# A convolution branch beside a gated MLP, forward and backward: loads and first products reordered, and the tap gradient's halo made by a shift product on TensorE

## Chip, cores and metric

One core of a Trainium2 chip. The metric is the device time of one execution in microseconds (us), lower is better. Time before: 2040.27 us (median of 3 runs, 2038.81 to 2040.48). A *ratio* is the recorded one of two kernels' runs in the same rounds on the same chip, so it is not quite the ratio of the medians that stand beside it, and can differ from that of the plain means in the fourth digit. Medians of different chips differ by some 4 us for the same kernel; the ratios do not carry that.

## The reference, cut

```python
def _A_ref(q, k, v, shift_k, ssm_k, ssm_D):            # "branch A"
    k_pad = jnp.pad(k, ((0, 0), (ks - 1, 0), (0, 0)))
    k_shift = sum over t of k_pad[:, t:t + S, :] * shift_k[:, ks - 1 - t]   # 4 taps
    kv = k_shift * v
    y = irfft(rfft(kv padded to 2S) * rfft(ssm_k padded to 2S))[:S]         # per channel
    y = y + kv * ssm_D
    return q * y

def _B_ref(x, W_gate, W_up, W_down):                   # "branch B", the MLP
    h = relu(x @ W_gate) * (x @ W_up)
    return h @ W_down

xn = _layernorm(x)                                     # over the last axis
out = x + _A_ref(xn, k, v, ...) + _B_ref(xn, ...)
# outputs: out, and the gradients of x, k, v, shift_k, ssm_k, ssm_D, W_gate, W_up, W_down
```

x, k, v are 2048 x 1024, the weights 1024 x 3584, all bf16. Of the gradients one matters here: that of `shift_k` needs, for each of the 4 taps, products of the gradient of `k_shift` with k moved by 0 to 3 positions, and the gradient of k needs the gradient of `k_shift` moved by 0 to 3 positions. A tile holds 16 positions per partition and three more, the **halo**, which belong to the next partition.

## The kernel before: the parts that matter

The MLP is a generator of TensorE work (in `hidden` each block of 512 columns is 24 products of 8 matmuls for half of the rows). Branch A is a second generator, in 8 groups of 128 channels; each `yield ns` says how much MLP work should pass before its next step. A scheduler then orders every engine's instructions by priority (`pri.now()` ahead of `pri.late()`); each engine executes its own list in that order.

```python
    def open(self):                                   # branch A's buffers
        self.ts = self.pool("a_ts", 3, side=R)        # three rotating work buffers: ttile()
        self.ps = self.pool("a_ps", 2, space=PSUM)    # two PSUM buffers for all of branch A
        ...
    def flip(self, src):                              # transposing copy: two halves on VectorE
        for c0 in range(0, 64, 32):
            self.pri.late()
            self.nc.vector.transpose(out=df[:, c0:c0 + 32, :], in_=sf[:, c0:c0 + 32, :])
        return dst
    ...
    def steps(self):
            ...
            yield from self.inv_b(Cg, gkv, 2000)      # gradient of kv
            gks = self.gradients(st, gkv, ksh)
            yield 6000
            yt = self.ttile("yt")
            yield from self.inv_b(Cy, yt, 2000)
            self.store_time(self.y_d, cg, yt)
            yield from self.inv_a(GH, 1800)           # last inverse step (GH,IA), ends in the flip
            Ch = self.flipped
            yield from self.grad_taps(gi, gks, kp, 1800)
            if nx is not None:
                self.loads_2(nx)
            yield 1500
            ghn = self.ttile("ghn")
            yield from self.inv_b_chan(Ch, ghn, 2000) # the flipped product (RB,flp)
    ...
    def gradients(self, st, gkv, ksh):
        gv = self.ttile("gv")
        self.tt(gv[:, 0:16, :], gkv[:, 0:16, :], ksh[:], ALU.mult)
        self.store_time(self.out_gv, cg, gv)
        gks = self.ttile("gks")
        self.tt(gks[:, 0:16, :], gkv[:, 0:16, :], vt[:], ALU.mult)
        pri.late()
        nc.gpsimd.memset(gks[:, 16:19, :], 0.0)                     # the halo:
        self.store(gks[0:64, 16:19, :], gks[64:P, 0:3, :])          # two SBUF-to-SBUF DMAs
        self.store(gks[64:P - 1, 16:19, :], gks[1:64, 0:3, :])
        gk = self.ttile("gk")
        self.taps(st, gk, gks, [(0, 0), (1, 1), (2, 2), (3, 3)])    # 7 passes of VectorE
        self.store_time(self.out_gk, cg, gk)
        return gks
    ...
    # the start
    b.ln_load(x, a.frm, "frm", 0)                     # first tile of x
    first = b.weights(B_W_gate, B_W_up, B_W_down, 0)  # 12 weight loads
    b.layer_norm(x, xn_d, a.frm, "frm", a.tmp, "tmp", a.sm)   # loads the rest of x, pieces of 3, 4, 4, 4
    with tc.issue_after(b.ln_act.ins), tc.issue_after(b.ln_dve.ins):
        a.tables()                                    # Fourier tables, at pri.now()
    ...
    a_steps, left = a.steps(), A_START                # cut: the loop that mixes both generators
```

## Time and profile before

| | before |
|---|---|
| time, median | 2040.27 us |
| span of the profiled execution | 2037.0 us |
| TensorE busy | 1930.9 us (95%) |
| next busiest engine, VectorE | 995.2 us (49%) |
| TensorE waits of the first 80 us: taps table, layer norm, VectorE's tables | 16.1 + 12.2 + 11.4 us |
| TensorE waits for the flip | 17.1 us |

The prediction below shows most of the lines. Two more, from the groups of instructions by shape (line, engine, operation, out<-in, shapes, count, then busy us and mean ns, then idle us of that engine just before them and what ended most of it):

```profile
L65 PE MATMUL ps<-RB,flp 128*128 128x64 bf16 x256 | 10.6, 203 | 16.9 <-DVE flp L281 16.6 <-DVE dg L73 0.2
L69 ACT CAST yt<-ps 128x1024 bf16<-128x1024 f32 x16 | 15.5, 1021 | 3.1 <-DMA out_dram<-gv 2.9
```

The first is the product that waits for the flip. The second is an eviction on ScalarE that waits for a store of `gv`. And the end of the MLP's first block, from TensorE's timeline (start us, length us, what):

```profile
91.38 3.62 PE L576 MATMUL ps_h<-wdT,goT 128*128 128x512 bf16 x15
94.83 3.62 PE L576 MATMUL ps_g<-wg,xnT 128*128 128x512 bf16 x16
```

`ps_g` at 94.83 is the second block's first product. "Block 0 ends at" always means this instant.

### The profile page before, as it was taken

The numbers are of one execution on the slowest core, as the hardware profiler recorded it, in microseconds if no ns is written. First come the engines' busy times: TensorE is split into PE (matmuls) and PEld (weight loads), VectorE is DVE, ScalarE is ACT, GpSimd is POOL, SyncE is SP. The second block draws the span as 40 slices with busy tenths as digits, with TensorE's granted clock in tenths as the row PEclk, the third lists the DMA queues.
The fourth block names the chain that finished last, engine by engine and source line by source line (L and its number), as shares of the span: only waits on it lengthen the run. The fifth ranks groups of instructions, "written<-read, shape, count | busy, mean of one in ns | idle before, by whom it ended". The sixth has DMA issues, their size and how long they took to land. (4 is left out here: it accounts for less than half of the span.)

```text
span 2037.0 us, 27072 instructions
## 1 busy us (share of the span) xinstructions
PE 1930.9 (95%) x10806; PEld 914.7 (45%) x11014; DVE 995.2 (49%) x1444; ACT 690.4 (34%) x902; POOL 20.1 (1%) x46
## 2 busy tenths in 40 slices
PE   4799999999999989999899999999989999999998
PEld 2345445444444445444444544444434444444443
DVE  4848578677687677565575740000112222223332
ACT  6456366356356347474655731111000000000000
POOL 1000000000000000000000000000000000000000
PEclk9899999999999999999999999999999999999999
DMA  9764666865565674545535269332899554454551
GB/s 266 203 160 125 160 159 172 196 174 169 156 167 161 167 192 135 152 131 153 179 119 162 73 169 334 106 119 83 182 257 233 150 134 114 114 126 119 122 128 45
DMA packets 616095, 319.10 MB, mean 157 GB/s; under 512 B 450080, under 2 KB 585248, under 8 KB 615968
## 3 DMA queue, kind: packets, MB, share of 16 engines
q1 hardware_dynamic: 614688, 313.16, 58.5%
q0 software_dynamic: 1280, 4.20, 0.6%
q8 instruction: 86, 1.41, 0.3%
q14 instruction: 41, 0.34, 0.1%
HBM read 141.36 MB, written 95.44 MB: 116 GB/s over the span
## 5 line engine op out<-in xcount | busy, mean ns | idle before, releaser
L673 PE MATMUL ps_w<-ugs,xn_nat 128*128 128x512 bf16 x1746 | 395.3, 380 | 2.7 <-issue 0.5
L673 PEld LDWEIGHTS <-xn_nat 128*128 128x128 bf16 x1792 | 171.5, 98 | 202.9 <-issue 7.1
L576 PEld LDWEIGHTS <-xnT 128*128 128x128 bf16 x1792 | 169.3, 98 | 201.2 <-issue 18.7
L576 PE MATMUL ps_h<-wdT,goT 128*128 128x512 bf16 x865 | 205.7, 382 | 13.4 <-DVE ru L634 11.4
L576 PE MATMUL ps_g<-wg,xnT 128*128 128x512 bf16 x875 | 207.8, 383 | 4.2 <-DVE ru L634 2.6
L576 PE MATMUL ps_u<-wu,xnT 128*128 128x512 bf16 x870 | 205.6, 380 | 1.7 <-issue 0.5
L673 PE MATMUL ps_d<-g_nat,hs 128*128 128x512 bf16 x866 | 203.1, 380 | 4.1 <-DMA ug_d<-ru 1.4
L757 PE MATMUL ps_o<-wd,hT 128*128 128x512 bf16 x878 | 195.0, 382 | 9.8 <-DMA hT<-h_d 8.9
L790 PE MATMUL ps_x<-wgT,ggT 128*128 128x512 bf16 x878 | 197.5, 379 | 1.0
L790 PE MATMUL ps_x<-wuT,guT 128*128 128x512 bf16 x878 | 197.3, 379 | 0.9
L759 DVE TENSOR_TENSOR o<-ps_o,ya 128x512 bf16<-128x512 f32 x32 | 21.5, 687 | 270.4 <-PE ps_o L757 269.8
L711 ACT CAST wi<-ps_w 128x512 bf16<-128x512 f32 x112 | 65.4, 585 | 255.8 <-PE ps_w L673 245.0
L757 PEld LDWEIGHTS <-hT 128*128 128x128 bf16 x896 | 87.7, 98 | 116.9 <-DMA hT<-h_d 10.8
L790 PEld LDWEIGHTS <-ggT 128*128 128x128 bf16 x896 | 87.6, 98 | 105.7
L790 PEld LDWEIGHTS <-guT 128*128 128x128 bf16 x896 | 87.6, 98 | 105.7
L576 PEld LDWEIGHTS <-goT 128*128 128x128 bf16 x896 | 84.9, 98 | 111.7 <-issue 20.2
L646 ACT CAST gh<-ps_h 128x512 bf16<-128x512 f32 x112 | 65.5, 586 | 202.5 <-PE ps_h L576 120.4
L792 DVE CUSTOM_DVE_ANT_0 gx<-ps_x,gy 128x512 f32<-128x512 f32 x32 | 22.1, 691 | 226.6 <-PE ps_x L790 212.5
L673 PEld LDWEIGHTS <-hs 128*128 128x128 bf16 x896 | 82.6, 98 | 98.7 <-issue 9.1
L281 DVE STREAM_TRANSPOSE flp<-B 128x1024 f32<-128x1024 f32 x48 | 90.1, 1934 | 47.8 <-ACT B L69 47.8
L634 DVE SCALAR_TENSOR_TENSOR ru<-ru,ps_u 128x512 bf16<-128x512 bf16 x112 | 76.0, 680 | 73.8 <-PE ps_u L576 47.9
L69 ACT CAST B<-ps 128x1024 bf16<-128x1024 f32 x96 | 95.6, 1020 | 36.0 <-PE ps L65 35.8
(152 smaller groups left out, 1707.9 us busy)
## 6 DMA issues: line engine op xcount, KB each, us to landing
ug_d<-ru SPq DMA_DIRECT2D x112, 256.0 KB, 3.4
ugs<-ug_d SPq DMA_DIRECT2D x112, 256.0 KB, 4.7
wg<-in_B_W_gate_dram SPq DMA_DIRECT2D x56, 256.0 KB, 3.4
wu<-in_B_W_up_dram SPq DMA_DIRECT2D x56, 256.0 KB, 4.6
h_d<-ht SPq DMA_DIRECT2D x112, 128.0 KB, 1.7
hs<-h_d SPq DMA_DIRECT2D x56, 256.0 KB, 4.4
out_dram<-wi SPq DMA_DIRECT2D x56, 256.0 KB, 2.1
gt<-in_grad_out_dram SPq DMA_DIRECT2D x32, 256.0 KB, 3.8
```

The source lines that it names most:

```text
L69: self.nc.scalar.copy(out=out, in_=in_)
L281: self.nc.vector.transpose(out=df[:, c0:c0 + 32, :], in_=sf[:, c0:c0 + 32, :])
L576: self.nc.tensor.matmul(ps[:], lhsT=xT[:, kt * P:(kt + 1) * P], rhs=w(kt), start=(kt == 0), stop=(kt == self.DT - 1))
L634: nc.vector.scalar_tensor_tensor(out=ru[s][:, 1, :], in0=ru[s][:, 0, :], scalar=0.0, in1=ps[:], op0=ALU.is_gt, op1=ALU.mult)
L646: nc.scalar.copy(out=gh[:], in_=ps[:])
L673: self.nc.tensor.matmul(ps[:], lhsT=lhsT(st), rhs=rhs(st), start=(st == 0), stop=(st == self.ST - 1))
L711: nc.scalar.copy(out=wo[:, d, :], in_=ps[:])
L757: nc.tensor.matmul(ps[:], lhsT=hT[:, kt, :], rhs=self.wd[:, kt, oc], start=(kt == 0), stop=(kt == self.FT - 1))
L759: nc.vector.tensor_tensor(out=o0[:, oc], in0=ps[:], in1=ya[:, oc], op=ALU.add)
L790: nc.tensor.matmul(ps[:], lhsT=T[:, kt, :], rhs=W[:, kt, oc], start=(i == 0), stop=(i == n - 1))
L792: V.tensor_tensor_reduce(out=gx[:, oc], in0=ps[:], in1=gy[:, oc], scale=1.0, scalar=0.0, op0=ALU.add, op1=ALU.add, accum_out=m[:, ob:ob + 1])
```

## The change

Intent: (1) at the start, issue loads and first products in the order in which they are needed, and give the table building low priority; (2) get the halo of the gradient of `k_shift` by a product with a shifted identity, instead of two DMAs, so that VectorE does not wait for them. Cut to its core:

```diff
     def tables(self):
-        pri.now()
+        pri.late()
 ...
+        self.NX = con.tile([P, P], BF16, name="NX")          # out[m] = in[m+64], from 64 on in[m-63]: the next 16 positions
+        V.tensor_copy(out=self.NX[:, 0:64], in_=self.identA[:, 64:P])
+        V.tensor_copy(out=self.NX[:, 64:P - 1], in_=self.identA[:, 1:64])
 ...
     def grad_taps(self, gi, gks, kp, ns):
-        ps = self.ps.tile([P, 4, 32], F32, name="ps6", tag="aps")
+        ps = self.ps.tile([P, 2, 512], F32, name="ps6", tag="aps")
+        self.mm(ps[:, 1, 0:3 * P], self.NX[:], gks[:, 0:3, :].rearrange("p r c -> p (r c)"))
+        self.act(gks[:, 16:19, :].rearrange("p r c -> p (r c)"), ps[:, 1, 0:3 * P])
 ...
     def steps(self):
             self.store_time(self.y_d, cg, yt)
+            yield from self.grad_taps(gi, gks, kp, 1800)
+            self.grad_k(st, gks)                 # the gk part of gradients(), now after yt
+            if nx is not None:
+                self.loads_2(nx)
             yield from self.inv_a(GH, 1800)
             Ch = self.flipped
-            yield from self.grad_taps(gi, gks, kp, 1800)
-            if nx is not None:
-                self.loads_2(nx)
-            yield 1500
+            yield 5000
             ghn = self.ttile("ghn")
 ...
     def gradients(self, st, gkv, ksh):
         self.tt(gks[:, 0:16, :], gkv[:, 0:16, :], vt[:], ALU.mult)
-        nc.gpsimd.memset(gks[:, 16:19, :], 0.0)
-        self.store(gks[0:64, 16:19, :], gks[64:P, 0:3, :])
-        self.store(gks[64:P - 1, 16:19, :], gks[1:64, 0:3, :])
-        gk = self.ttile("gk")
-        self.taps(...)
 ...
-    LN_CHUNKS = (1, 3, 4, 4, 4)
+    LN_CHUNKS = (1, 1, 2, 4, 4, 4)
 ...                                              # block 0: gate and up products of the first two
+                ahead = fb + half == 0           # tiles come ahead of the first down product
 ...
-    b.ln_load(x, a.frm, "frm", 0)
-    first = b.weights(B_W_gate, B_W_up, B_W_down, 0)
+    load(0)
+    first = [b.col_block(B_W_gate, 0, "wg")]
+    load(1)
+    first.append(b.col_block(B_W_up, 0, "wu"))
+    load(2)
+    load(3)
+    first.append(b.row_block_T(B_W_down, 0, "wdT"))
+    goT = [b.load_T(g, i, "goT") for i in range(4)]
+    load(4)
+    a.load_shift()
+    load(5)
```

Also in it, cut here: the table of square roots is loaded by an activation at the very start, the transpose of the filter taps moves to the start of branch A, and one product of branch A (`gt * xt`) is made later.

## The prediction

> **What bounds the kernel now.** I read the page's table of engines first, then the slices, the waits of TensorE, and the timeline of the stretches where TensorE is idle.
>
> ```profile
> PE 1930.9 (95%) x10806; PEld 914.7 (45%) x11014; DVE 995.2 (49%) x1444; ACT 690.4 (34%) x902; POOL 20.1 (1%) x46
> ...
> PE   4799999999999989999899999999989999999998
> ```
>
> TensorE is busy for 95% of 2037 us; no other engine passes half. Only what shortens TensorE's idle time can pay, and that is 2037.0 - 1930.9 = 106 us at most. About 200 of the 11014 matmuls have no record (10806 against 11014 weight loads; at 0.216 us each, 8 in 1.73 us in the chain, up to 45 us), so the true idle time is nearer 65 to 90 us. The waits and the timeline say where:
>
> ```profile
> PE ps L65 <- DVE flp L281: 17.1, 9, 2.9
> PE ps_sk L205 <- DMA sk_b<-in_A_shift_k_dram: 16.1, 1, 16.1
> PE pst_x L600 <- DVE ln_x L558: 12.2, 2, 10.3
> PE ps_h L576 <- DVE ru L634: 11.4, 2, 10.5
> PE ps_o L757 <- DMA hT<-h_d: 8.9, 4, 3.1
> PE ps L65 <- ACT H L69: 6.0, 7, 2.0
> ...
> 10.35 1.03 PE L600 MATMUL pst_x<-ident,ln_x 128*128 128x128 bf16 x8 [10.35 <-DVE ln_x L558]
> 27.47 0.29 PE L205 MATMUL ps_sk<-identA,sk_b 128*32 128x128 bf16 x1 [16.09 <-DMA sk_b<-in_A_shift_k_dram]
> ...
> 30.41 5.95 PE L576 MATMUL ps_g<-wg,xnT 128*128 128x512 bf16 x16
> ...
> 79.21 0.59 PE L576 MATMUL ps_h<-wdT,goT 128*128 128x512 bf16 x1 [10.51 <-DVE ru L634]
> ```
>
> (columns of a wait: total us, times, longest; of the timeline: start, length, what, the wait before it). Three places concern the change. **The start**: the first real product begins at 30.4 us; before it there are only transposes. The wait charged to the taps table (16.1 us) is not the cause alone: the second piece of x is issued at 12.65 us, behind twelve weight loads, lands at 18.8, and its layer norm ends at 30.3. **At 69 to 79 us** VectorE makes tables for 10 us without a break while two finished products wait for it. **From 200 to 1207 us**, where the convolution branch runs beside the MLP, 28 us of waits remain, 17.1 of them for the flip. The tail (last product at 2028.5) and the 8.9 us for hT are not touched by the change.
>
> **What the Trainium skill says.** "Perfetto Trace Analysis", Identifying the Most-Contended Engine and Optimization Strategy: TensorE's busy share is a poor measure because matmuls are pipelined; look for gaps on the contended engine and for what releases them. The trace agrees: records last 380 ns but come every 216. "ScalarE: Activation LUTs", What ACT_TABLE_LOAD costs: about 1283 ns a load. The trace has 1.28 us three times. "TensorE: Matmul & The Clock Gate", Part 1: after some microseconds of idle the array restarts at half clock. The trace agrees: the first 16 gate matmuls took 5.95 us, later 16 take 3.62, and the stretch 70:80 was granted 0.63. "DMA: Bandwidth & Descriptors", Latency and other measured facts: a DMA has about 2 us of fixed cost. The halo copy in the chain took 2.19 us, but its wait is longer, below.
>
> **Part 1, loads and first products in order of need.** x comes in pieces of 1, 1, 2, 4, 4, 4 tiles; the new issue order is x0, gate, x1, up, x2, x3, down, four goT, x4, x5. The square-root table is loaded while x0 is in flight: its 1.28 us started at 6.72 us in the chain of the first tile, of which about 0.8 is saved. What the diff hides is in the built order of each engine. VectorE copies the first two transposed tiles only after the layer norm of x0, x1 and x2; and ScalarE's first relu comes after all 16 reductions of x0 to x3 and four of x4. So I follow these two queues with durations of the trace (ScalarE 1.04 us a pass over a tile; VectorE 0.43 per tile and subtraction or scaling, about 0.2 per small operation, eight of them after the root).
>
> - x0 lands at 3.48 as before and is normalised at about 9.5; x1 passes through both queues behind it, until 14.7.
> - x2: 3 MB lie ahead of its end. At 250 GB/s (the first two slices have 266 and 203, the first 10 us 253) that is 12 us plus 2 of latency: 14. Two passes on ScalarE to 16.2, subtract, two passes to 19.5, one pass over x3 put between, root at 20.7, eight small operations to 22.3, scaling to 23.2, first copy at 23.9. **The first gate product starts at about 24 us**, not 11 as the new order of loads suggests, against 30.4.
> - Four products of eight matmuls, the first ones cold: to 33.4. The next transposes need a bank that only the relu frees, at 34 to 35. Their copies stand behind the subtraction of x4 and the evictions of the up products: 39.1. So a second gap of about 5 us.
> - From 39 us the block has 20 products of 1.73 us left, 34.6 us, plus some 6 us for two more pairs of transposes behind layer-norm work. The tables are now cut up: MLP operations stand between pieces of at most 1.34 us (2.3 for one), so the 10.5 us gap goes. **Block 0 ends at about 80 us.**
>
> Before, its last products ran from 91.38 to 94.8, and that included 2.0 us of filter transposes now done later. Gain: 94.8 - 2.0 - 80 = **12.8 us**, all on the path, as TensorE is the bound from there on.
>
> **Part 2, the halo.** Removed, eight times: a memset on GpSimd, two SBUF-to-SBUF copies, and VectorE's wait for them:
>
> ```profile
> DVE tap L73 <- DMA gks<-gks: 51.9, 7, 20.7
> ...
> 249.79 0.85 SPq L85 DMA_DIRECT2D gks<-gks  x1
> ...
> 253.24 0.88 SPq L85 DMA_DIRECT2D gks<-gks  x1
> ...
> 255.60 1.23 DVE L73 TENSOR_TENSOR tap<-gks,skb 128x2048 bf16<-128x2048 bf16 x1 [1.06 <-DMA gks<-gks]
> ...
> 265.40 1.88 DVE L281 STREAM_TRANSPOSE flp<-C 128x1024 f32<-128x1024 f32 x1
> ...
> 267.33 1.89 PE L65 MATMUL ps<-RB,flp 128*128 128x64 bf16 x32 [2.65 <-DVE flp L281]
> ```
>
> VectorE's 51.9 us of waiting are not on the path as such: it is 49% busy. The path is their consequence. gks is ready at 226, but the copies are issued only at 249.8 and 253.2, in a queue shared with other traffic; the tap sums then crowd in front of the two flips, and TensorE waits for the second flip. By shapes, 16.6 of the 17.1 us are before this one product (7 or so groups, some 2.3 us each). In the new order the two flips stand ahead of most tap sums, and 24 to 40 MLP matmuls (5 to 9 us) lie between the last inverse step and the flipped product, where 5 to 39 lay before, mostly about 18. I take 14 of the 16.6 as gained. The crowding of convolution steps with 0 to 3 matmuls between them, which gives the ScalarE waits (H 6.0, others near 5), moves to other groups and is a little less: 2 us gained.
>
> Added: eight matmuls of 128x384, 0.216 x 384/512 = 0.16 us and a weight load of 0.10: 2 us at most, 1.5 as they overlap. Their evictions on ScalarE (about 0.5 us each, from 0.6 at 512 columns) lie beside other work on an engine that is 34% busy. The new product waits for gks, with about 60 matmuls (13 us) between its cause and it: no stall. **Sum of part 2: -14 - 2 + 1.5 = -14.5 us.**
>
> Total: 2040.3 - 12.8 - 14.5 = **2013 us**.
>
> **Rivals.** (a) The early start is worth far more: products begin at 11 or 12 us, as x0, x1 and the gate weights are there by 8. For it: the intent, and the flips stand first on TensorE. Against: the built VectorE order. It would gain 10 to 13 us more: about 2001. (b) The start gains nothing, because layer norm on ScalarE (32 passes of 1.04, 33 us, plus relus) or the load of x4 behind eight transposing DMAs bounds both kernels, and waiting moves from before 30 us to 33 to 56. The queues above leave only a few us of slack; then the start gives 3 to 5 us: about 2022. (c) The flip waits are not due to the halo but to the crowding of the scheduler's order; then another wait (ghn's eviction waiting for the last tap sum, or the shift product's bank, shared with the tap product in two buffers, held until ScalarE and VectorE have both read it) takes their place: part 2 gives 3 us, the time is about 2024. (d) Later transfers hide the gain: A finishes earlier or later, but it had 230 us to spare before the weight gradients end at 1437, so this costs nothing.
>
> **Range and chances.** The start is uncertain by some 6 us either way, part 2 by 6 and rearrangement elsewhere by 5: together 10, so 80% lie within about 12 to 13: **2001 to 2027 us**. Faster by over 2% means under 1999.5, 41 us, nearly all the idle time touched here (30 + 12 + 28, less a start that cannot be below 11): chance 0.09. Slower by 2% would take a new stall in every group: 0.01. Within 2%: 0.90.
>
> **What would show it.** Right, if: the first gate product stands at 22 to 26 us with an idle gap of 4 to 8 us near 34 to 39; block 0 of the MLP ends at 76 to 84; no 10 us wait of ps_h on VectorE; the wait of the flipped product is under 4 us in total; no DMA wait before the taps; eight NX products of about 0.2 us without a wait. Wrong, if the gate starts near 12 (then a), or if ScalarE or x4's DMA holds TensorE for over 10 us between 30 and 60 (b), or if waits of the convolution products from 200 to 1200 us still sum to over 20 us (c).

## The result, and the profile after

The changed kernel took **2011.27 us** (median of 4 runs, 2010.59 to 2014.13) beside 2040.38 for the kernel before on the same chip: ratio 0.9861, 95% interval 0.9844 to 0.9879. That is "within 2%", and the predicted 2013.0 is 1.7 us from it. Run again later on another chip (below) the ratio was 0.9848 (0.9832 to 0.9865).

The page after: engines, and TensorE's busy share by fortieth of the span.

```profile
PE 1944.6 (97%) x11022; PEld 916.2 (46%) x11022; DVE 996.6 (50%) x1460; ACT 694.6 (35%) x912; POOL 16.3 (1%) x36
...
PE   3999999999999999999999999999999999999998
```

The slice of 7 tenths and three of 8 have become 9. Busy time *rose* by 13.7 us mainly because this trace has a record of all 11022 matmuls: a later trace of the same kernel (e14 below), with 10817 records, is busy for 1927.8 us. What TensorE waited for:

```profile
PE ps_g L595 <- DVE xnT L621: 11.4, 4, 6.8
...
PE pst_x L619 <- ACT ru L645: 6.1, 1, 6.1
PE ps_o L789 <- DMA hT<-h_d: 5.9, 3, 2.6
...
PE ps L65 <- DVE flp L291: 2.5, 3, 1.3
```

The flip's 17.1 us became 2.5, and the 11.4 us of `ps_h` on VectorE do not occur. The start, from the timeline of both engines concerned:

```profile
24.10 5.67 PE L595 MATMUL ps_g<-wg,xnT 128*128 128x512 bf16 x16 [6.84 <-DVE xnT L621]
...
34.40 1.06 ACT L554 ACTIVATE ln_j<-ln_x 128x1024 bf16<-128x1024 bf16 x1 [4.58 <-DMA ln_x<-in_A_q_dram]
...
38.66 1.05 ACT L645 ACTIVATE ru<-ps_g 128x512 bf16<-128x512 f32 x2
...
39.29 1.86 PE L619 MATMUL pst_x<-ident,ln_x 128*128 128x128 bf16 x16 [6.06 <-ACT ru L645]
...
43.48 6.21 PE L595 MATMUL ps_g<-wg,xnT 128*128 128x512 bf16 x16 [2.33 <-DVE xnT L621]
...
84.93 3.62 PE L595 MATMUL ps_g<-wg,xnT 128*128 128x512 bf16 x16
```

The first gate product stands at 24.10 us (before: 30.41). Then a second gap: ScalarE waits 4.58 us for the fifth piece of x, the relus stand behind its four passes, and only the relus free the PSUM banks for the next transposes. Block 0 ends at 84.93. The product after the flip, and the eight new shift products:

```profile
L65 PE MATMUL ps<-RB,flp 128*128 128x64 bf16 x256 | 10.1, 193 | 1.6 <-DVE flp L291 1.5
...
L65 PE MATMUL ps<-gks,NX 128*128 128x384 bf16 x8 | 2.6, 326 | 0.0
```

From three instants of both timelines the span's 27.6 us (2037.0 to 2009.4) divide as follows. Before, block 0 also held 2.0 us of filter transposes, which the change moves past it; they are taken out of the first row and put into the second.

| stretch | before | after | gain | predicted |
|---|---|---|---|---|
| start to end of block 0 | 94.83 - 2.0 | 84.93 | 7.9 | 12.8 |
| to the end of the weight gradients | to 1437.05 | to 1412.66 | 16.5 | 14.5 |
| output phase to the end | 600.0 | 596.7 | 3.2 | 0 |

The total is right to 2 us partly because misses have opposite signs (-4.9, +2.0, +3.2), which is luck. The first row is also a late case: in six other traces of the same start (e1, e3, e12, e4, e14, e17) block 0 ends at 81.6 to 82.9, a gain of 10.0 to 11.3. And 16.5 in the second row says *where*, not *why*.

### The profile page after: what moved, and what is told of

It reads as the page before. It is cut to its first block, busy times and chain, and to the rows that moved or that the text cites. A ratio compares the mean times of both kernels' runs of the same rounds, so it can differ in the third digit from the quotient of the medians. Undisturbed runs are those within 1.5% of the kernel's fastest.

```text
span 2009.4 us, 27247 instructions
## 1 busy us (share of the span) xinstructions
PE 1944.6 (97%) x11022; PEld 916.2 (46%) x11022; DVE 996.6 (50%) x1460; ACT 694.6 (35%) x912; POOL 16.3 (1%) x36
## 4 chain that ended last, share of the span: by engine, by line
PE 47%; ACT 2%; DMA 1%; SPq 1%; issue 0%; DVE 0%; DVEq 0%
PE ps_x L822 19%; PE ps_w L705 17%; PE ps_o L789 8%; PE ps L65 1%; DMA hT<-h_d 1%; ACT G L69 1%; SPq L781 0%; ACT H L69 0%; ACT K L69 0%; ACT wi L743 0%; ACT B L69 0%; SPq L758 0%; PE pst L280 0%; DVE gx L837 0%; DVE gm L834 0%
## 5 line engine op out<-in xcount | busy, mean ns | idle before, releaser
L705 PE MATMUL ps_w<-ugs,xn_nat 128*128 128x512 bf16 x1792 | 400.2, 379 | 1.1 <-DMA xn_nat<-xn_d 1.0
L595 PE MATMUL ps_g<-wg,xnT 128*128 128x512 bf16 x896 | 213.6, 387 | 15.4 <-DVE xnT L621 11.4
L705 PE MATMUL ps_d<-g_nat,hs 128*128 128x512 bf16 x896 | 208.6, 381 | 3.6 <-DMA hs<-h_d 3.6
L69 ACT CAST C<-ps 128x1024 bf16<-128x1024 f32 x96 | 96.7, 1016 | 48.4 <-PE ps L65 48.4
```

Of the source, the lines that this page charges most:

```text
L69: self.nc.scalar.copy(out=out, in_=in_)
L595: self.nc.tensor.matmul(ps[:], lhsT=xT[:, kt * P:(kt + 1) * P], rhs=w(kt), start=(kt == 0), stop=(kt == self.DT - 1))
L705: self.nc.tensor.matmul(ps[:], lhsT=lhsT(st), rhs=rhs(st), start=(st == 0), stop=(st == self.ST - 1))
```

## The experiments

**Theory** (the prediction's): VectorE's wait for the halo copies pushes the tap sums in front of the flips; the shift product removes it. **Rivals:** the flip waits come from the scheduler's order and the buffers' rotation, so it is the reordering that pays and the shift product is beside the point; and, for the start, that x's later pieces and layer norm bound it. Twelve runs; the ratio is always to the kernel before in the same rounds. All outputs are right.

| run | what it is | median us (lowest to highest) | ratio [95%] | flip wait us | block 0 ends |
|---|---|---|---|---|---|
| e1_start_only | part 1 alone | 2032.69 (2026.70-2034.56) | 0.9947 [0.9934, 0.9960] | 17.5 | 82.5 |
| e2_halo_only | part 2 alone | 2020.54 (2018.93-2023.82) | 0.9894 [0.9881, 0.9907] | 1.1 | 98.4 |
| e3_order_dma_halo | all but the shift product | 2013.71 (2012.01-2016.44) | 0.9860 [0.9847, 0.9872] | 3.1 | 82.9 |
| e12_gk_after_yt | e1 + gk after yt | 2024.35 (2023.59-2025.34) | 0.9911 [0.9896, 0.9925] | 14.0 | 82.5 |
| e4_shift_old_order | e1 + shift product, old order | 2024.53 (2019.19-2028.85) | 0.9934 [0.9920, 0.9949] | 18.6 | 81.6 |
| e6_tables_now | change, tables at high priority | 2018.27 (2017.27-2019.40) | 0.9903 [0.9891, 0.9916] | 2.4 | 90.9 |
| e5_x4_early | change, fifth piece of x earlier | 2007.34 (2006.97-2010.19) | 0.9853 [0.9840, 0.9865] | 2.9 | 80.1 |
| e10_products_first | change, layer norm staged behind products | 2007.50 (2003.74-2011.02) | 0.9850 [0.9837, 0.9864] | 2.5 | 84.5 |
| e14_after_again | the change, unaltered | 2008.31 (2005.22-2009.22) | 0.9848 [0.9832, 0.9865] | 1.4 | 82.2 |
| e17_room_before_flip | e12 + one number | 2007.53 (2007.00-2009.52) | 0.9845 [0.9830, 0.9859] | 2.4 | 81.6 |
| e13_products_first_gp_store | e10 + early stores issued by GpSimd | 1997.47 (1995.14-1997.78) | 0.9791 [0.9776, 0.9806] | 1.1 | 71.4 |
| e15_products_first_gp_store_x4 | e13 + e5 | 1997.17 (1995.45-1998.17) | 0.9791 [0.9777, 0.9806] | 2.4 | 72.2 |

The first four shared one chip (before there: 2042.25), the next four a second (2038.13), the last four a third (2041.08).

### The two halves

`e1_start_only`: the change with the whole halo part (grad_taps, gradients, the order of the steps) as before.

> Part 1 alone: the changed start, with the halo by two copies and the old order of the group's tail. In the trace of the changed kernel block 0 of the MLP ends at 84.9 us against 92.8 before (94.8 less 2.0 of filter transposes moved to later), so the start is worth 7.9 us. Theory (the two parts are independent): 2040.4 - 7.9, a time of 2030 to 2034 us, block 0 ending at 84 to 86, and waits of TensorE for the flip between 200 and 1210 us of 12 to 20 us as before. Rival (the start shifts the branch against the MLP, and that is what thinned the later waits): under 2027 us, flip waits under 8 us.

`e2_halo_only`: the kernel before with the halo part alone.

> Part 2 alone: the old start (with the identity matrix shared, which frees the memory needed), the shift product and the new order of the tail. From the two traces the stretch from the end of block 0 to the end of the weight gradients is 14.5 us shorter although 2.0 us of transposes moved into it, so part 2 should be worth 16.5 us, and 3.1 us came in the output phase, which neither part touches. Theory (independent parts): 2040.4 - 16.5 = 2024, less up to 3 if the output phase's gain belongs to part 2: 2020 to 2025 us, the gap near 70 to 79 us still there. Rival (part 2 gains only with the new start): over 2030 us.

Measured: the start alone gives 0.53%, part 2 alone 1.06%, together 1.59%; the whole change 1.39% and, on another chip, 1.52%. So the parts add, near enough. The 12.0 us of `ps_h` on VectorE stay in e2 and go in e1; the flip's waits stay in e1 (17.5) and go in e2. Each wait belongs to the half it was assigned to. (Block 0 of e1 ended at 82.5, earlier than the expected 84 to 86, which came from the late trace.)

### Is it the shift product?

`e3_order_dma_halo`: the changed kernel, but the halo made by DMA as before.

```diff
-        self.mm(ps[:, 1, 0:3 * P], self.NX[:], gks[:, 0:3, :]...)
-        self.act(gks[:, 16:19, :]..., ps[:, 1, 0:3 * P])
+        self.nc.gpsimd.memset(gks[:, 16:19, :], 0.0)             # in gradients(), as before
+        self.store(gks[0:64, 16:19, :], gks[64:P, 0:3, :])
+        self.store(gks[64:P - 1, 16:19, :], gks[1:64, 0:3, :])
```

> The changed kernel with the shift product taken out again: halo by memset and two copies as before, everything else (order of the tail, yt before gk, wider gap before the last product) as changed. Theory O (the order and the rotation of the three work buffers made the gain, since yt took the buffer of gv and its eviction waited for the late store of gv): within 3 us of the changed kernel, 2008 to 2014 us, waits for the flip under 5 us, although VectorE waits for the halo copies 30 us or more. Rival D (the prediction's: VectorE's wait for the halo copies is what pushed the flips): 2020 to 2026 us with flip waits of 10 us or more.

`e4_shift_old_order`: the reverse. The shift product is there, but `gk` before `yt`, the taps after the inverse step and the 1500 are as before.

```diff
             gks = self.gradients(st, gkv, ksh)
-            yield 6000
+            yield 3000
+            self.shift_halo(gks)          # NX product and its eviction alone
+            self.grad_k(st, gks)
+            yield 3000
```

> Part 1 plus the shift product alone: the halo comes from TensorE right after gks, gk is summed at once as before (so gk is allotted before yt, and yt takes the buffer of gv), tap product after the inverse step, short gap. Theory O (rotation of the buffers): yt's eviction still waits for the late store of gv, the inverse steps and the last product stay bunched (1 to 4 and 5 to 8 matmuls between them in the built order), so the time is that of part 1 alone within 4 us, 2029 to 2036 us, with flip waits over 10 us. Rival D (halo copies were the cause): 2013 to 2020 us, flip waits under 5 us.

Waits of e3, then of e4:

```profile
DVE gk L73 <- DMA out_dram<-gv: 24.6, 5, 11.7
...
PE ps L65 <- DVE flp L287: 3.1, 3, 2.7
...
DVE tap L73 <- DMA gks<-gks: 0.3, 1, 0.3
...
PE ps L65 <- DVE flp L291: 18.6, 9, 2.4
```

Measured: e3 has the ratio of the change itself (0.9860 beside 0.9861 and 0.9848), flip waits of 3.1 us, and VectorE waits for its halo copies 0.3 us in all, where it waited 51.9. (Its tap sums now wait 24.6 us at their start for the store of `gv`, and the copies land meanwhile; the flips do not suffer from that either.) e4 removes the wait for the copies from VectorE just as well (4.1 us for ScalarE's eviction of the halo instead) and still has 18.6 us of flip waits; `yt`'s eviction waits 9.3 us for the store of `gv`, as expected of it. Its time fell between the two expectations; its ratio differs from that of e1, on another chip, by 0.0013, within the intervals. **Taking the halo copies away is neither enough for the gain (e4) nor needed for it (e3), and the shift product is worth nothing that these runs can show.** This refutes the theory.

### Then what in the reordering?

`e12_gk_after_yt`: part 1, halo by DMA, and of part 2 only that `gk` is made after `yt`.

```diff
+            self.grad_k(st, gks)          # was inside gradients(), before yt
             yield from self.inv_a(GH, 1800)
```

> Part 1 alone plus one move: the sum gk is made after yt has been evicted, so that yt takes the buffer of gkv (free after gks) and not that of gv (free only after its store). Halo by copies, tap product after the inverse step and the short gap as before. Theory O: the inverse steps are spread again (8 matmuls between them in the built order, where 1 to 4 stood), yt's eviction shows no wait for the store of gv, flip waits fall below 8 us, time 2013 to 2022 us. Rival D (halo copies): as part 1 alone within 3 us, about 2032 us.

Why that could matter, in the trace of the kernel before (first group; SPq is a DMA issue in SyncE's queue):

```profile
224.85 0.64 SPq L85 DMA_DIRECT2D out_dram<-gv  x1
...
249.06 0.64 SPq L85 DMA_DIRECT2D out_dram<-gv  x1
...
253.40 1.93 ACT L69 CAST yt<-ps 128x1024 bf16<-128x1024 f32 x2 [2.93 <-DMA out_dram<-gv]
```

Three work buffers rotate. With the order gkv, gv, gks, gk, yt, the fourth and fifth take the buffers of gkv and gv, so `yt` waits until gv has been stored; and that store, low in priority, had its second half issued 24 us after the first. The products for `yt` had begun at 231.19 and 235.30; their PSUM buffers, both that branch A has, stayed full until 253.4, and the inverse steps behind them came late and bunched: in all eight groups they ran within 3.3 to 3.8 us, in e12 within 5.4 to 8.9. ScalarE is seen waiting for this store in one group only; otherwise the eviction simply stands late in its list. With gk last, `yt` takes gkv's buffer, which is free. In e12 `yt` no longer waits for the store of gv (VectorE now waits for it, 9.4 us, before gk), the wait for H falls from 6.0 to 2.2, and the ratio improves from 0.9947 to 0.9911. But 14.0 us of flip waits remain, so this move is a part, about 0.36% or 7 us, not the whole, and both expectations missed: the flip waits were to fall below 8 us, or the time to stay near 2032. The same line also moves the tap sums themselves; that it is the buffer that counts is argued, not shown.

`e17_room_before_flip`: e12 with one number changed.

```diff
             if nx is not None:
                 self.loads_2(nx)
-            yield 1500
+            yield 5000
```

> The kernel with part 1, the halo by DMA and gk made after yt (which had 0.9911 and 14.0 us of flip waits), with one number changed: the budget of MLP work between the last inverse step and the flipped product is 5000 ns instead of 1500. In the built order 24 to 40 MLP matmuls now stand before that product in every group, where 8 to 39 stood. If that room is what takes the flip wait away, the wait falls under 4 us and the time is that of the changed kernel (ratio 0.986, within 0.002). If the order of the tap product before the inverse step is what does it, or the tap sums of VectorE still crowd in front of the flips, 8 us or more of flip waits stay and the ratio is near 0.990.

`e14_after_again`: the changed kernel itself, in the same rounds.

> The changed kernel unaltered, in the rounds of the next three, to compare with directly. Ratio to before 0.986 as measured (about 2011 us if before is 2040).

Measured: e17 has 0.9845 and the change 0.9848, with intervals of 0.0015 either way. **That one number, with gk after yt, gives the whole gain of part 2**: the flip waits fall from 14.0 to 2.4. Neither the shift product nor the tap product ahead of the inverse step is needed for it. What the number does, in the third group. First e12 (timeline; the last inverse product ended at 542.27):

```profile
543.35 2.00 DVE L287 STREAM_TRANSPOSE flp<-C 128x1024 f32<-128x1024 f32 x1 [0.29 <-ACT C L69]
...
552.99 1.22 DVE L73 TENSOR_TENSOR tap<-gks,skb 128x2048 bf16<-128x2048 bf16 x1
554.12 1.90 DVE L287 STREAM_TRANSPOSE flp<-C 128x1024 f32<-128x1024 f32 x1
...
556.08 0.64 PE L65 MATMUL ps<-RB,flp 128*128 128x64 bf16 x16 [2.56 <-DVE flp L287]
```

and e17 (last inverse product ended at 549.66):

```profile
551.71 1.96 DVE L287 STREAM_TRANSPOSE flp<-C 128x1024 f32<-128x1024 f32 x1
...
554.64 1.21 DVE L73 TENSOR_TENSOR tap<-gks,skb 128x2048 bf16<-128x2048 bf16 x1
555.76 1.93 DVE L287 STREAM_TRANSPOSE flp<-C 128x1024 f32<-128x1024 f32 x1
...
560.97 0.63 PE L65 MATMUL ps<-RB,flp 128*128 128x64 bf16 x16
```

In e12 six of the seven operations of the tap sum stand between the two halves of the flip, which ends 13.7 us after the last inverse product. In e17 four stand before the first half and two between, the flip ends after 8.0 us, and the product comes 3.3 us later still. So the number works in two ways: it puts 24 to 40 MLP matmuls ahead of the flipped product in every group (counted from the tap product), where e12 had 8 to 39, and it moves the scheduler's placing of the tap sums. In this group the matmuls between are nearly the same (39 and 40), and it is VectorE's order that differs; in others the room differs as well.

The traces of all eight groups show that either alone makes a wait. In e4 no tap operation stands between the halves of the flip, and the flipped product starts 4.9 to 5.4 us after the last inverse product: that is what the eviction and two half flips take. But only 7 to 10 MLP matmuls come between (1.5 to 2.2 us at 216 ns), and every group waits 2.1 to 2.4 us. In e12 the four groups with three to six tap operations between the halves wait 2.4 to 2.7 us each, although 22 to 47 matmuls follow the last inverse product there; the other four wait 0.4 us at most. e17 has three or more between the halves in one group, which waits 1.9 us. So the room has to cover the flip, as 24 matmuls do (5.2 us), and the halves have to stay together. Two things are not shown: why the budget also moved the tap sums, and whether it would do without `gk` after `yt`, as 5000 in the old order was not run.

### The start

`e6_tables_now`: the change, with the tables at high priority again (`pri.late()` back to `pri.now()`, one line).

> The changed kernel with the sine tables at immediate priority again. Theory (the priority is what removed the 10.5 us gap): a wait of 7 to 11 us on VectorE comes back between 55 and 85 us and the time is 2018 to 2022 us. Rival (the new order of the products alone would have spread them, or TensorE has two pairs of work ahead): within 3 us of 2011.

Measured: block 0 ends at 90.9, a wait of 9.0 us for VectorE is back (in front of the transposes of the fourth pair), ratio 0.9903. Low priority of the tables is worth about 0.4 to 0.55%, 8 to 11 us. That is nearly all that the start gives: e6 is no faster than e2, which has part 2 with the old start (0.9903 beside 0.9894, on another chip), although its first gate product comes at 22.9 us. The new order of loads and first products alone gains nothing that these runs show. Low priority in the old order was not run.

`e5_x4_early`: the fifth piece of x is issued ahead of W_down and grad_out.

```diff
     load(3)
+    load(4)
     first.append(b.row_block_T(B_W_down, 0, "wdT"))
     goT = [b.load_T(g, i, "goT") for i in range(4)]
-    load(4)
```

> The changed kernel with the load of x4 issued before the down weights and the four goT. In the changed kernel ScalarE waits 4.6 us for x4 (it lands at 34.4), with the root of x3 and the first relus behind it. Theory (this wait holds the second gap): relus about 4 us earlier, second gate pair at 39 to 40 instead of 43.5, 2006 to 2010 us. Rival (the queue of layer norm work holds it anyway, or the down weights now come late): within 2 us of 2011.

Measured: the second gap is gone (next gate pair at 37.02 instead of 43.48) and block 0 ends at 80.1, the figure of the prediction's sum, though by other parts: the first gate product came at 25.2 us (22.7 and 22.9 in e4 and e6 on the same chip), the second pair earlier, and the fourth pair waited 3.87 us. Ratio 0.9853: its interval overlaps those of the change, so no more than a possible gain.

`e10_products_first`: layer norm is made a generator, and its later pieces are put behind the first transposes, products and relus in every engine's list.

```diff
+                    xT += [self.flip_xn(0), self.flip_xn(1)]
+                    with self.tc.issue_after(self.copied.ins):
+                        self.norm(2)
                     yield from gate_up(0)
+                    with self.tc.issue_after(self.relu.ins):
+                        self.norm(2)
```

> The changed kernel with the layer norm cut in stages: the copies of the first two transposed tiles stand before the second half of x2's norm, the first relus before the squares of x3, x4 behind the relus of the second pair, x5 behind those of the third. Same instructions, another order on ScalarE and VectorE. Theory (order of the two queues, not data, holds the start): first gate product at 18 to 20 us, second pair at 29 to 33 instead of 43.5, block 0 ends at 68 to 73 instead of 84.9, time 1996 to 2001 us. Rival (loads bound the start: down weights and goT land too late for h, or weights of block 1 do): first gate at 19 but block 0 ends after 78, time over 2004 us.

Measured: the first gate products at 17.22 us and the second at 29.02, 7 and 14 us earlier than in the change; and then nothing of it is left at the end of block 0 (84.5), ratio 0.9850. Its timeline says where it went:

```profile
42.73 4.97 SPq L658 DMA_DIRECT2D h_d<-ht  x2
...
47.91 0.59 ACT L667 CAST gh<-ps_h 128x512 bf16<-128x512 f32 x1 [8.60 <-DMA h_d<-ht]
...
49.88 5.96 PE L598 MATMUL ps_g<-wg,xnT 128*128 128x512 bf16 x16 [9.43 <-DVE xnT L624]
...
84.51 5.70 PE L598 MATMUL ps_g<-wg,xnT 128*128 128x512 bf16 x16 [5.24 <-ACT gh L667]
```

`ht` and `gh` share three buffers. ScalarE's eviction of the first down product waits 8.60 us for a store of `ht`, which stands in SyncE's queue behind loads of the next block's weights and of branch A (the gate loads alone hold it for 7.63 us); VectorE's product and copies wait in turn, and TensorE 9.43 us. At the block's end TensorE waits 5.24 us more: the last eviction stands behind 4.07 us of table building on ScalarE and then waits 2.99 us for another store of `ht`. The gain turned into new waits; so the expected rival had the outcome right (84.5, over 2004 us), but not by its cause.

`e13_products_first_gp_store`: so the stores of the first two blocks go out from GpSimd's queue, which is nearly idle.

```diff
+                early = nc.gpsimd if half == 0 and fb < 2 else nc.sync
 ...
-                        nc.sync.dma_start(out=h_d[...], in_=ht[:])
+                        early.dma_start(out=h_d[...], in_=ht[:])
 ...
-                        nc.sync.dma_start(out=ug_d[...], in_=ru[s][:])
+                        early.dma_start(out=ug_d[...], in_=ru[s][:])
```

> The products-first start (layer norm of later pieces staged behind the first products), with the stores of the first two blocks' results issued from GpSimd instead of SyncE. If SyncE's order of issue is what held ScalarE's eviction (8.60 us of waiting for a store, 9.43 us of TensorE idle before the third pair of gate products), both waits fall under 3 us, block 0 ends at 72 to 78 instead of 84, and the ratio is 0.979 to 0.982 (about 1997 to 2003 us). If the store itself is slow because the DMA engines are full of weight loads, the wait stays at 5 us or more and the ratio stays at 0.985.

```profile
40.71 3.63 PE L598 MATMUL ps_g<-wg,xnT 128*128 128x512 bf16 x15 [0.41 <-DVE xnT L624]
...
71.43 5.30 PE L598 MATMUL ps_g<-wg,xnT 128*128 128x512 bf16 x16 [3.50 <-ACT gh L668]
```

Measured: the third pair of gate products comes 9 us earlier than in e10, ScalarE's wait for these stores falls from 11.6 to 3.0 us, block 0 ends at 71.4 (its last product at 67.9; one wait of 3.50 us remains between). **1997.47 us, ratio 0.9791 to the kernel before; its mean is 0.5 to 0.6% below the change's in the same rounds. It beats both kernels.**

`e15_products_first_gp_store_x4`: e13 with the loads of e5.

> As the run before, with the fifth piece of x issued ahead of the transposed loads of W_down and grad_out. If x4 then still bounds the third and fourth pair, another 2 to 4 us come off: block 0 ends at 69 to 74, ratio 0.977 to 0.981. If the down products then wait for their later weights instead, it is no better than the run before.

Measured: the same as e13 (0.9791). With the products ahead of layer norm the fifth piece of x no longer stands in the way (in e13 ScalarE shows no wait for it), so loading it earlier gains nothing.

## Why the prediction was right, and where not

**First gate product at about 24 us, not 11: right** (24.10, and 22.54 in e14). Following the built order of VectorE and ScalarE, not the order of loads, gave it. e10 confirms the reason: with layer norm behind the products they start at 17.22.

**Second gap: right in place and kind, mis-sized.** The step was "The next transposes need a bank that only the relu frees, at 34 to 35", with x4 as "the subtraction of x4" in a queue, not as a load. The relus began at 38.66, because ScalarE first waited 4.58 us for x4. The second gate pair started at 43.48 instead of 39.1, 4.4 late; from there to the end of block 0 it took 41.5 us for the 41 of the sum (its first 16 matmuls ran at the slow clock, 6.21 us, but fewer us went to later transposes than allowed). So block 0 ended at 84.93, outside 76 to 84 by 0.9, and the start gave 7.9 instead of 12.8. That trace is the latest of seven: the others end at 81.6 to 82.9, inside the range, and still show ScalarE waiting 3.7 to 4.1 us for x4. So some 1.5 to 3 us of the miss remain there; the rest was chance in that trace. The missing term stood in rival (b), "the load of x4 behind eight transposing DMAs": with x4 loaded earlier (e5) this wait and the second gap are gone. Its size for the start, 3 to 5 us, is too small (part 1 alone: 0.53%, 11 us).

**No 10 us of `ps_h` on VectorE: right**, and e6 shows that the tables' priority did it. What the sum did not see is that this priority, and not the earlier first products, is nearly the whole gain of the start.

**The idle time "nearer 65 to 90 us": too low.** It counts 0.216 us for each missing record. The two traces of the changed kernel, with 11022 and 10817 records, differ by 16.8 us of busy time, 0.08 us a record; so the 208 missing ones hide some 17 us, and about 90 us were idle.

**Part 2, -14 for the flip: right in size** (17.1 to 2.5). The crowding gave more than the 2 us allowed: the waits for H, K, C, B and G were 6.0 + 1.3 + 1.8 + 1.1 us of those listed before and 1.3 + 1.5 + 1.3 + 1.0 after, 5.1 less. The eight shift products wait for nothing; their records last 2.6 us in all, but the next product starts 0.16 us after one (in the first group), so the predicted 1.5 to 2 is not contradicted. The wait of the tap sums for the halo is gone, but "no DMA wait before the taps" is not quite what came: VectorE now waits 12.5 us before gk for the store of gv, whose buffer gk takes.

**Part 2, the cause: wrong.** The failed step reads "The path is their consequence": copies issued late, tap sums crowding in front of the flips for their sake. e4 took the copies away and the flips waited 18.6 us; e3 kept the copies and they waited 3.1. Half of the step held: in e4 no tap operation holds up either half of a flip any more. It was not enough, because only 7 to 10 matmuls cover the 5 us that the flip takes. The prediction had that in its next sentences, the room of 24 to 40 matmuls before the flipped product, but counted it as part of the halo's gain. Rival (c) had the cause, "the crowding of the scheduler's order", right, and the conclusion wrong: since the change alters that order, the wait did not merely move. The buffer rotation, with `yt` waiting for a late store, is in neither; the line for it stood in the profile before with 2.9 us, which looked too small to matter. What it held was the PSUM; how much of the gain that explains is not shown.

**Nothing after 1437 us: a miss of 3.2 us.** The wait for hT fell from 8.9 to 5.9 us. It is between 4.3 and 8.2 us in the twelve runs, 6.6 in e1 and 6.5 in e2, so it belongs to no one part; why is left open.

Rival (a), products at 11 or 12 us, was rightly set aside for this kernel. Rival (d) has no sign in any run.

## What to carry to other kernels

When a diff brings a mechanism and an order together, run the order without the mechanism and the mechanism without the order before crediting either: here one constant and one line moved carried all of a gain that was meant for a new instruction. Give a product that depends on a chain of other engines as much room as that chain takes: here about 5 us. And when an earlier start gains nothing, follow the new wait to its queue: a store behind loads that are not yet needed gave back 14 us here, and another engine's queue returned most of them.

## What the Trainium skill lacked or had wrong

- "DMA: Bandwidth & Descriptors", Issuing engines are not separate DMA queues, says that issuing from several engines only saves the sequencer's time for starting a transfer, usually small. Here it was not small: three gate loads held SyncE's queue for 7.63 us (e10), and a store stood behind them. Issuing the stores from GpSimd took ScalarE's wait for them from 11.6 to 3.0 us and the ratio from 0.9850 (e10) to 0.9791 (e13, another chip). The skill does advise one engine for loads and another for stores ("Perfetto Trace Analysis", DMA Optimizations), but neither page gives what a store behind loads can cost.
- "Perfetto Trace Analysis", Optimization Strategy, offers too few SBUF or PSUM buffers for a bubble that repeats. The bubble of 0.8 to 3.0 us in each group may fit that in part: making gk after yt, which also frees the right buffer, gave 0.36%. The page lacks the other cause found here, the placing of instructions by a scheduler: with the same number of buffers one budget took the bubbles from 14.0 to 2.4 us.
- "TensorE: Matmul & The Clock Gate", Part 1, has nothing wrong here: it puts the return to the slow clock after about 3.4 us of idle, in a window that runs freely. 16 matmuls took 5.30 us after a gap of 3.50 us (e13), 5.31 after one of 3.87 us (e5), and 3.63 us after one of 1.84 us (the changed kernel), with 3.62 when warm. But in e15 the first 8 after a gap of 3.88 us took 1.89 us, the warm rate: a gap of that length may or may not cost.
